# A new step table for the attention's planner, and another place for three pieces of VectorE's and ScalarE's work in the second feed-forward layer

## The chip, the cores and the metric

One core of one Trainium2 chip runs the whole program. The metric is the device time of one execution in microseconds (us), as the median of three runs. Beside it stands one profiled execution, whose trace tells when each instruction of each engine ran: PE is TensorE's matrix multiplications, PEld its weight loads, DVE is VectorE, ACT is ScalarE, POOL is GpSimd and SP is SyncE, which issues DMAs here.

## What is computed

A block-causal attention on 4 x 8 heads of 576 tokens, then two feed-forward layers on the 2304 x 512 result. The second layer multiplies its hidden values by their own cosine. Everything is float32.

```python
# attention, B, H, S, D = 4, 8, 576, 64; key blocks of 64 up to the query's own
scores = np.where(block_i >= block_j, q @ k.T / sqrt(D), -1e9)
attn = exp(scores - max(scores)); attn /= sum(attn) + 1e-9
x = (attn @ v).transpose(0, 2, 1, 3).reshape(2304, 512)
# first layer, 512 -> 2048 -> 512
g = relu(x @ w_in) ** 2;  x = g @ w_out
# second layer, 512 -> 2048 -> 512
h = x @ w2_in;  out = (h * cos(h)) @ w2_out
```

## The kernel before

**Attention (to 150.5 us in the trace).** The heads go in 16 pairs, and two pairs make one round, called Q below (8 rounds). The order of the work is not written out: `class Plan` (L56 on) holds every step with its engine, an assumed cost, a rank and what it waits for, and sends the steps out one by one, in each case the one that can start soonest, and among equals the one with the lowest rank. The rank is the pair's number on a scale plus an entry of the table `RANK`, with one row for each kind of step and five columns for early, middle and late pairs. PE's products come in three forms of its array, named by the planner's `mode`: "quarters" (64 x 64; the scores at L440 and the scores of the last key block, L488), "all" (128 x 128; the transposes of P at L601 and of the last block's PL at L628) and "columns" (128 x 64; P transposed times the values, L656). `SWITCH` and `STAY` are what the planner adds for a change of form. In one steady round PE does scores, last scores (16 products at L488), a product with 20 matmuls at L656, then the transposes of the next pairs.

**First layer.** Blocks of tokens go through x @ w_in (L1128), the squares (L1005 to L1008) and the outputs (L1062), 8 steps to a block. Its last blocks also split the second layer's weights from float32 into parts; that work is called `convert` (DVE: L285, L268, L291, L310, L279; ACT: L261, L307, L274).

**Second layer.** Four blocks of 512 tokens, each 8 steps (r = 0 to 7), and one last block of 256 tokens. Each step forms its hidden values with seven products of half the width (L997), in the order 11, s2, s1, 12, s3, 22, s4, into three PSUM banks (bank_a, bank_b, bank_c; h0, h1 and h2 in the listings). ACT copies the first product to `p1` (L1182), and DVE adds: `u2` = s2's bank plus p1, then c22 (twice), c21 and c12 (all L1185). bank_b is used by s2, s3 and 22 in turn, so PE's s3 waits until u2 has been taken out of it. Between the seven products lie 24 matmuls of the outputs (L1064) for an earlier step's waves.

The waves of a step run through DVE and ACT in halves 1 and 0: `count` (ACT, L1017), a first range step `less` (DVE, L1020), a second one `rest` (DVE, L1020 again), `size` (ACT, L1025), `cosine` (ACT, L1028), `times` (DVE, L1031), `high` (ACT, L1034) and `low` (DVE, L1037), whose result `gs` feeds the outputs. In `second_layer` count, less and rest are issued at a step's end, and size to low in the next step. In block 1 of this layer `convert` is still running, one turn a step.

At the end of a block of the first layer `finish` copies the four accumulators into `xall`, in turn by ACT and DVE (L1079); the first outputs of the second layer need those banks. The second layer's accumulators go to DRAM by way of a tile `o` (four copies by ACT, L1095). The casts and sums that make the next block's operands (`prepare`; its casts by ACT at L960) are spread over a block's steps. In the very last block ACT and DVE each copy one half of an accumulator (L1085), and DMAs carry it out (L1087, L1090).

Of the kernel before, what the change touches and what calls it, by code (L numbers as in the profile page):

```python
# [28 lines left out]
    "load": (82.8, 1611.6, 1657.9, 3246.6, 954.3),  # L29
    "k scale": (-832.1, -930.8, -388.4, 136.8, -501.4),  # L30
    "scores": (-558.9, 281.0, 420.5, -1133.4, -1153.0),
    "maximum": (1445.5, 700.8, 1063.1, 903.2, 737.5),
    "exponential": (-486.4, -1482.8, -125.1, 162.5, -1193.8),
    "last": (184.8, 21.8, 2059.4, 1402.4, 2295.1),
    "maximum last": (2758.6, 929.9, 2619.1, 1994.3, 2109.6),
    "exponential last": (1969.8, 2274.9, 3555.7, 1382.3, 1535.7),
    "guard": (-2663.2, -2893.3, -2702.3, -868.9, -2289.9),
    "invert": (-262.4, -573.8, -174.1, 303.8, -626.9),
    "scale": (-2043.2, -104.9, -614.7, 400.0, -1131.2),
    "guard last": (-1325.7, -1081.9, -491.4, -1263.7, -1854.2),  # L40
    "invert last": (236.2, 753.5, 476.9, 965.6, 609.5),
    "scale last": (679.6, -403.4, 136.8, 510.8, -90.6),
    "turn": (466.2, 1248.8, -506.4, 902.5, 824.5),
    "turned": (2175.2, 2205.7, 1749.8, 1390.3, 1533.7),
    "turn last": (-2697.6, -2953.5, -3175.8, -2666.8, -2239.3),
    "turned last": (-553.6, -1082.6, 956.0, -65.3, -20.2),
    "lesser": (-1876.9, -1222.0, -913.7, -1060.9, -1794.0),
    "value load": (-3600.7, -827.7, -2460.7, -3001.3, -2351.0),
    "weighted": (-371.1, -843.8, -605.9, 170.3, -119.5),
    "keep": (-891.0, -537.2, -248.1, -248.9, 1171.0),  # L50
    "weights": (2361.2, 4005.7, 2327.2, 3114.2, 2407.8),
# [4 lines left out]
class Plan:  # L56
# [7 lines left out]
    SWITCH = 0.15  # L64
    STAY = 0.261
# [37 lines left out]
    def emit(self):  # L103
# [16 lines left out]
        for _ in self.steps:  # L120
            best = None
            for engine, mine in able.items():
                times, rooms = {}, {}
                for n in mine:
# [6 lines left out]
                    if mode not in (None, tiling):  # L131
                        times[n] = max(times[n], clock[engine] + self.SWITCH) + self.STAY
# [43 lines left out]
def tile_block_causal_attention__then__two_ffn(  # L176
# [12 lines left out]
    nc = tc.nc  # L189
# [172 lines left out]
    def attention():  # L362
        with ExitStack() as actx:
# [67 lines left out]
            def add_scores(p, m):  # L431
# [4 lines left out]
                def product():  # L436
# [9 lines left out]
                    "P", max(0.18, (n - 64) / 600), ("scores", rank), product,  # L446
# [30 lines left out]
            def add_last(Q):  # L477
# [5 lines left out]
                for y in range(2):  # L483

                    def product(y=y):
# [8 lines left out]
                        "P", 2 * S / 2400, ("last", rank + y / 4), product, keys, [f"SL{Q}.{y}", f"free{r}.L"],  # L494
# [186 lines left out]
            def add_half(n):  # L681
# [6 lines left out]
                plan.add("A", 0.56, rank, x.shift, late, [raw])  # L688
                plan.add("V", 0.45, rank, x.mask, [high] + late, [bits], **both)
# [57 lines left out]
    def layers():  # L747
# [329 lines left out]
        def finish(layer, t0, n, a, end):  # L1077
# [4 lines left out]
            if end:  # L1082
                o = raw_p.tile([128, DM], F32, tag="raw", name="o")
                for copy, own in zip(copies, halves):
                    copy(out=o[:, own], in_=accs[a][:, own])  # L1085
                if a < n // 128 - 1:
                    nc.sync.dma_start(out=rows, in_=o)  # L1087
                    return
                for queue, own in zip((nc.scalar, nc.sync), halves):
                    queue.dma_start(out=rows[:, own], in_=o[:, own])  # L1090
                return
# [23 lines left out]
        def run(*keys):  # L1115
            for key in keys:
                if late:
                    late[key]()
# [54 lines left out]
        def second_layer(s, i, r):  # L1173
# [17 lines left out]
            run(("size", 1), ("size", 0), ("cosine", 1), ("cosine", 0))  # L1191
            times("s2", "t2", bank_b, True)
            plus(u2, bank_b, p1)
            run(("times", 1),)
# [13 lines left out]
            elif not (loads or loaded or begun) and r < half - 1 and i + 1 < len(blocks):  # L1208
                if r >= 1 and not todo and ready[0] < i:
# [9 lines left out]
            pop(len(pend) - per - 3)  # L1219
            times("22", "t4", bank_b, False)  # L1220
# [10 lines left out]
            if (loads or loaded or begun) and r == 1:  # L1231
                convert()
# [96 lines left out]
```

## Time and profile before

| | us |
|---|---|
| median of three runs (lowest, highest) | 940.26 (939.94, 942.24) |
| the profiled execution's own time | 940.51 |
| its span, first to last instruction | 938.0 |
| PE busy | 923.5 (98%) |
| DVE busy | 666.1 (71%) |
| ACT busy | 616.2 (66%) |
| attention from PE's start of its steady part to its end | 17.6 to 150.5 |
| second layer, block 1 | 537.1 to 627.9 |
| second layer, blocks 2, 3 and 4 | 627.9 to 885.9 |
| last block and the way out | 885.9 to 938.0 |

The span leaves out 2.5 us of the execution. PE is busy nearly throughout, so the time is PE's work plus the idle stretches in front of single PE instructions; these are what the rows further down look for. A busy DVE or ACT matters only where PE stands waiting at the end of what they do.

### The profile page before, as it was taken

The numbers are of one execution on the slowest core, as the hardware profiler recorded it, in microseconds if no ns is written. First come the engines' busy times: TensorE is split into PE (matmuls) and PEld (weight loads), VectorE is DVE, ScalarE is ACT, GpSimd is POOL, SyncE is SP. The second block draws the span as 40 slices with busy tenths as digits, with TensorE's granted clock in tenths as the row PEclk, the third lists the DMA queues.
The fourth block names the chain that finished last, engine by engine and source line by source line (L and its number), as shares of the span: only waits on it lengthen the run. The fifth ranks groups of instructions, "written<-read, shape, count | busy, mean of one in ns | idle before, by whom it ended". The sixth has DMA issues, their size and how long they took to land.

```text
span 938.0 us, 15762 instructions
## 1 busy us (share of the span) xinstructions
PE 923.5 (98%) x5818; PEld 783.1 (83%) x5818; DVE 666.1 (71%) x1386; ACT 616.2 (66%) x1328; POOL 93.6 (10%) x204
## 2 busy tenths in 40 slices
PE   7999999999999999999999999999999999999998
PEld 4777778888888888888888888889899889899897
DVE  6988997777786556655477567777776777666654
ACT  7987898887886556655568745565555555645564
POOL 4867741000000000000000000000000000000000
PEclk9999999999999999999999999999999999999999
DMA  8434303667665766776554754445454545554462
GB/s 308 145 134 155 120 30 112 202 206 259 202 202 199 259 237 226 242 249 228 198 180 181 265 205 156 160 158 202 171 198 182 202 165 193 184 212 157 136 217 75
DMA packets 41308, 176.12 MB, mean 188 GB/s; under 512 B 4240, under 2 KB 9616, under 8 KB 34064
## 3 DMA queue, kind: packets, MB, share of 16 engines
q1 hardware_dynamic: 40512, 174.41, 53.5%
q8 instruction: 45, 0.74, 0.3%
q10 hardware_dynamic: 720, 0.72, 0.2%
q14 instruction: 31, 0.25, 0.1%
HBM read 145.23 MB, written 29.88 MB: 187 GB/s over the span
## 4 chain that ended last, share of the span: by engine, by line
PE 89%; DVE 6%; ACT 3%; DMA 1%; issue 1%; POOL 0%; SPq 0%; ACTq 0%; DVEq 0%; POOLq 0%
PE acc L1064 18%; PE h L1128 14%; PE h L997 14%; PE acc L1062 13%; PE h L855 7%; PE acc L879 5%; PE ps L440 4%; PE ps L656 4%; PE ps L601 4%; PE h L1243 2%; PE h L879 2%; DVE g L1020 1%; DMA kB<-in_kT_dram 1%; PE ps L488 1%; DVE ha L1185 1%
## 5 line engine op out<-in xcount | busy, mean ns | idle before, releaser
L1064 PE MATMUL acc<-w,gs 128*128 128x512 f32 x864 | 221.0, 393 | 0.9 <-ACT o L1095 0.9
L1064 PEld LDWEIGHTS acc<-w,gs 128*128 128x128 f32 x864 | 153.2, 189 | 27.5 <-DVE gs L1037 1.3
L1062 PE MATMUL acc<-gs,w 128*128 128x512 f32 x576 | 138.9, 389 | 0.0
L1128 PE MATMUL h<-xs,ws 128*128 128x512 f32 x576 | 137.8, 389 | 0.0
L1128 PEld LDWEIGHTS h<-xs,ws 128*128 128x128 f32 x576 | 108.1, 188 | 22.3
L1062 PEld LDWEIGHTS acc<-gs,w 128*128 128x128 f32 x576 | 107.7, 188 | 21.9
L1008 DVE TENSOR_TENSOR gs<-ha,gs 128x512 fp32r<-128x512 f32 x48 | 33.2, 692 | 90.2 <-ACT gs L1007 90.2
L997 PE MATMUL h<-w,ws 128*128 128x256 f32 x480 | 70.8, 283 | 4.1 <-DVE u L1185 2.4
L997 PEld LDWEIGHTS h<-w,ws 128*128 128x128 f32 x480 | 65.4, 189 | 10.4 <-DVE u L1185 4.6
L1037 DVE TENSOR_TENSOR gs<-g,gs 128x512 fp32r<-128x512 f32 (+1 forms) x80 | 48.2, 635 | 32.3 <-ACT gs L1034 32.2
L307 ACT CAST w<-bits 128x512 fp32r<-128x512 f32 x64 | 39.9, 624 | 45.5 <-DVE bits L285 45.5
L855 PE MATMUL h<-xs,w 128*128 128x512 f32 (+1 forms) x384 | 68.9, 335 | 0.0
L855 PEld LDWEIGHTS h<-xs,w 128*128 128x128 f32 x384 | 59.6, 188 | 7.9
L1031 DVE TENSOR_TENSOR g<-ha,g 128x512 f32<-128x512 f32 x64 | 43.9, 687 | 29.9 <-ACT g L1028 29.9
L1017 ACT ACTIVATE turns<-ha 128x512 int32<-128x512 f32 x64 | 37.3, 626 | 41.1 <-DVE ha L1185 40.6
L1005 ACT ACTIVATE ha<-h 128x512 f32<-128x512 f32 x48 | 28.5, 593 | 50.0 <-PE h L1128 50.0
L1025 ACT ACTIVATE g<-g 128x512 f32<-128x512 f32 (+1 forms) x80 | 45.1, 588 | 22.6 <-DVE g L1020 22.6
L1182 ACT COPY ha<-h 128x256 f32<-128x256 f32 x32 | 11.9, 372 | 62.7 <-DVE g L1031 59.4
L1028 ACT ACTIVATE g<-g,half_pi 128x512 f32<-128x512 f32 (+1 forms) x80 | 50.5, 670 | 0.5
L1020 DVE SCALAR_TENSOR_TENSOR g<-turns,ha 128x512 f32<-128x512 int32 x64 | 41.6, 689 | 10.7 <-ACT turns L1017 10.7
L1020 DVE SCALAR_TENSOR_TENSOR g<-turns,g 128x512 f32<-128x512 int32 (+1 forms) x80 | 48.0, 633 | 0.6
L1185 DVE TENSOR_TENSOR ha<-h,u 128x256 f32<-128x256 f32 x96 | 37.8, 420 | 13.0 <-PE h L997 11.3
(170 smaller groups left out, 1715.7 us busy)
## 6 DMA issues: line engine op xcount, KB each, us to landing
raw<-in_w_dram SPq DMA_DIRECT2D x64, 512.0 KB, 4.4
qB<-in_qd_dram SPq DMA_DIRECT2D x15, 576.0 KB, 5.2
ws<-parts1.0_2025 SPq DMA_DIRECT2D x4, 1792.0 KB, 7.3
ws<-parts1.1_2026 SPq DMA_DIRECT2D x4, 1792.0 KB, 7.3
ws<-parts1.2_2027 SPq DMA_DIRECT2D x4, 1792.0 KB, 7.3
ws<-parts1.3_2028 SPq DMA_DIRECT2D x4, 1792.0 KB, 8.4
ws<-parts1.4_2029 SPq DMA_DIRECT2D x4, 1792.0 KB, 7.3
ws<-parts1.5_2030 SPq DMA_DIRECT2D x4, 1792.0 KB, 7.2
```

The costliest lines, as they stand in the source:

```text
L855: nc.tensor.matmul(h, lhsT=w[:, a, kk * 128 : (kk + 1) * 128], rhs=xs[kk].parts[:, y], start=(m == 0), stop=(m == 3 * KD - 1),)
L879: nc.tensor.matmul(accs[a][:, 0:n], lhsT=w[:, x, a * 128 : (a + 1) * 128], rhs=gs[:, y], start=(c == 0 and m == 0 and a % shared == 0), st ...
L997: nc.tensor.matmul(bank[:, 0:n], lhsT=w[:, c : c + 128], rhs=own[two][:, y, k, 0:n], start=(start and k == 0 and i == 0), stop=(k == 1 and ...
L1020: nc.vector.scalar_tensor_tensor(out=own, in0=turn, scalar=-part, in1=start, op0=ALU.mult, op1=ALU.add)
L1025: nc.scalar.activation(out=own, in_=own, func=AF.Abs)
L1028: nc.scalar.activation(out=own, in_=own, func=AF.Sin, bias=half_pi, scale=-1.0)
L1031: nc.vector.tensor_tensor(out=own, in0=h, in1=own, op=ALU.mult)
L1037: nc.vector.tensor_tensor(out=to[:, 1], in0=own, in1=to[:, 0].bitcast(F32), op=ALU.subtract)
L1062: nc.tensor.matmul(accs[a][:, 0:n], lhsT=w[:, y, sl], rhs=gs[:, z, x, 0:n], **flags)
L1064: nc.tensor.matmul(accs[a], lhsT=gs[:, y, x, sl], rhs=w[:, z], **flags)
L1128: nc.tensor.matmul(h[:, 0:n], lhsT=w[:, c : c + 128], rhs=xs[kk].parts[:, y], start=(m == 0), stop=(m == 3 * KD - 1),)
L1185: nc.vector.tensor_tensor(out=to, in0=bank[:, 0:m], in1=what, **add)
```

## The change

It has five parts.

1. `RANK` gets new numbers throughout, `SWITCH` becomes a table by pair of forms, `STAY` becomes 0, and the assumed costs of the scores, the last scores, and two of convert's steps are altered. PE's order is the same up to 17.6 us. After that its changes of form go from 49 to 54.
2. In block 1 of the second layer (`i == last + 1`) u2's addition is issued ahead of `rest`. In the later blocks the code moves too, but the order on every engine stays.
3. In step r = 1 of that block `convert` is issued ahead of product 22 and its addition c21, where it had been at the step's end.
4. `prepare` for the last, smaller block begins at r = 2 of block 4, not r = 1.
5. In the last block the two halves of an accumulator go into two tiles of their own, with a DMA each.

```diff
-    SWITCH = 0.15
-    STAY = 0.261
+    SWITCH = {("quarters", "columns"): 0.45, ("quarters", "all"): 0.28, ("all", "quarters"): 0.1,
+              ("all", "columns"): 0.25, ("columns", "all"): 0.12, ("columns", "quarters"): 0.12}
+    STAY = 0.0
...
-    "scores": (-558.9, 281.0, 420.5, -1133.4, -1153.0),
+    "scores": (-876.3, 699.6, 689.0, 88.7, -607.6),
...
-                    "P", max(0.18, (n - 64) / 600), ("scores", rank), product,
+                    "P", (0.18, 0.33, 0.538, 0.751)[m], ("scores", rank), product,
...
         def finish(layer, t0, n, a, end):
...
-                o = raw_p.tile([128, DM], F32, tag="raw", name="o")
-                for copy, own in zip(copies, halves):
-                    copy(out=o[:, own], in_=accs[a][:, own])
...
+                parts = [pool.tile([128, DM // 2], F32, tag=tag, name="o") for pool, tag in ((raw_p, "raw"), (bits_p, "bits"))]
+                for copy, own, o in zip(copies, halves, parts):
+                    copy(out=o, in_=accs[a][:, own])
+                for queue, own, o in zip((nc.scalar if a == n // 128 - 1 else nc.sync, nc.sync), halves, parts):
+                    queue.dma_start(out=rows[:, own], in_=o)
...
         def second_layer(s, i, r):
...
             times("11", "11", bank_a, True)
             copy(p1, bank_a)
-            run(("size", 1), ("size", 0), ("cosine", 1), ("cosine", 0))
+            if i > last + 1:
+                run(("rest", 1), ("rest", 0))
+                run(("size", 1), ("size", 0), ("cosine", 1), ("cosine", 0))
             times("s2", "t2", bank_b, True)
             plus(u2, bank_b, p1)
+            if i == last + 1:
+                run(("rest", 1), ("rest", 0))
+                run(("size", 1), ("size", 0), ("cosine", 1), ("cosine", 0))
             run(("times", 1),)
...
-                if r >= 1 and not todo and ready[0] < i:
+                if r >= (1 if blocks[i + 1][2] > 256 else 2) and not todo and ready[0] < i:
...
             pop(len(pend) - per - 3)
+            if (loads or loaded or begun) and r == 1:
+                convert()
             times("22", "t4", bank_b, False)
             plus(c21, bank_b, p1)
...
-            run(("count", 1), ("less", 1), ("count", 0), ("less", 0), ("rest", 1), ("rest", 0))
+            run(("count", 1), ("less", 1), ("count", 0), ("less", 0))
             ws.append(stream(s + 2))
-            if (loads or loaded or begun) and r == 1:
-                convert()
```

VectorE's order in a steady step of block 1, from c21 and c12 (the two additions into ha that close a step) to the first `times` (L1031 before, L1032 after); u1 is u2, and the two rows at L1020 (L1021 after) are less and rest. Before:

```order
L1185 TENSOR_TENSOR ha_2033<-h1_2042,u0_3352 128x256
L1185 TENSOR_TENSOR ha_2033<-h2_2043,u1_3353 128x256
L1020 SCALAR_TENSOR_TENSOR g_2034<-turns_2035,ha_2033 128x512 x2
L1020 SCALAR_TENSOR_TENSOR g_2034<-turns_2035,g_2034 128x512 x2
L1185 TENSOR_TENSOR u1_3353<-h1_2042,u0_3352 128x256
L1031 TENSOR_TENSOR g_2034<-ha_2033,g_2034 128x512
```

The same stretch of VectorE in the changed kernel:

```order
L1183 TENSOR_TENSOR ha_2033<-h1_2042,u0_3352 128x256
L1183 TENSOR_TENSOR ha_2033<-h2_2043,u1_3353 128x256
L1021 SCALAR_TENSOR_TENSOR g_2034<-turns_2035,ha_2033 128x512 x2
L1183 TENSOR_TENSOR u1_3353<-h1_2042,u0_3352 128x256
L1021 SCALAR_TENSOR_TENSOR g_2034<-turns_2035,g_2034 128x512 x2
L1032 TENSOR_TENSOR g_2034<-ha_2033,g_2034 128x512
```

The addition u1 has moved ahead of the two second range steps.

VectorE in step r = 1 of the same block, from the first accumulator copy into xall to the next step's u1. Before:

```order
L1079 COPY xall_60<-acc1_2046 128x512
L1185 TENSOR_TENSOR ha_2033<-h1_2042,u0_3352 128x256
L1079 COPY xall_60<-acc3_2048 128x512
L1185 TENSOR_TENSOR ha_2033<-h2_2043,u1_3353 128x256
L1020 SCALAR_TENSOR_TENSOR g_2034<-turns_2035,ha_2033 128x512 x2
L1020 SCALAR_TENSOR_TENSOR g_2034<-turns_2035,g_2034 128x512 x2
L285 SCALAR_TENSOR_TENSOR bits_5262<-raw_5169,bits_5262 128x512
L268 TENSOR_SCALAR bits_5438<-raw_5211 128x512
L291 TENSOR_SCALAR raw_5169<-bits_5262 128x512
L310 SCALAR_TENSOR_TENSOR w1_5440<-raw_5169 128x512
L279 SCALAR_TENSOR_TENSOR raw_5211<-raw_5211 128x512
L1185 TENSOR_TENSOR u1_3353<-h1_2042,u0_3352 128x256
```

The same stretch in the changed kernel:

```order
L1080 COPY xall_60<-acc1_2046 128x512
L286 SCALAR_TENSOR_TENSOR bits_5262<-raw_5169,bits_5262 128x512
L269 TENSOR_SCALAR bits_5412<-raw_5211 128x512
L292 TENSOR_SCALAR raw_5169<-bits_5262 128x512
L311 SCALAR_TENSOR_TENSOR w1_5414<-raw_5169 128x512
L280 SCALAR_TENSOR_TENSOR raw_5211<-raw_5211 128x512
L1183 TENSOR_TENSOR ha_2033<-h1_2042,u0_3352 128x256
L1080 COPY xall_60<-acc3_2048 128x512
L1183 TENSOR_TENSOR ha_2033<-h2_2043,u1_3353 128x256
L1021 SCALAR_TENSOR_TENSOR g_2034<-turns_2035,ha_2033 128x512 x2
L1183 TENSOR_TENSOR u1_3353<-h1_2042,u0_3352 128x256
L1021 SCALAR_TENSOR_TENSOR g_2034<-turns_2035,g_2034 128x512 x2
```

Convert's five instructions now stand ahead of c21 and of the copy of the accumulator acc3. On ACT, convert's three instructions have moved ahead of the two counts in the same way.

PE in one of four steady rounds of the attention, from the last scores on (ps are PSUM banks, PT the transposed P, ident the identity that transposes). Before:

```order
L488 MATMUL ps1_87<-kB1_99,qB1_97 64x288 x2
L488 MATMUL ps2_88<-kB1_99,qB1_97 64x288 x2
L656 MATMUL ps4_90<-PT_106,vB0_100 64x320 x6
L656 MATMUL ps4_90<-PT_106,vB0_100 64x192 x2
L656 MATMUL ps4_90<-PT_106,vB0_100 64x64 x2
L601 MATMUL ps0_86<-ident_94,P1_103 128x128 x3
L601 MATMUL ps3_89<-ident_94,P1_103 128x128 x2
L601 MATMUL ps5_91<-ident_94,P1_103 128x128 x3
```

The same place in the changed kernel:

```order
L489 MATMUL ps1_87<-kB1_99,qB1_97 64x288 x2
L489 MATMUL ps2_88<-kB1_99,qB1_97 64x288 x2
L602 MATMUL ps4_90<-ident_94,P1_103 128x128 x3
L602 MATMUL ps5_91<-ident_94,P1_103 128x128 x2
L657 MATMUL ps0_86<-PT_106,vB0_100 64x320 x6
L657 MATMUL ps0_86<-PT_106,vB0_100 64x192 x2
L657 MATMUL ps0_86<-PT_106,vB0_100 64x64 x2
L602 MATMUL ps3_89<-ident_94,P1_103 128x128 x3
```

Five transposes have moved between the last scores and the product with the values, so the round has one change of form more: quarters to all to columns to all, where it was quarters to columns to all.

## Rows read from the trace of the kernel before

**Rows 1.** Windows: stretch, its length, each engine's busy time, clock, DMA share, GB/s.

```profile
17.60:44.40 26.80, 26.43 (x275) 17.84 (x274) 24.83 (x71) 24.67 (x84) 20.10 (x43) 1.00 0.52 184
44.40:62.00 17.60, 17.11 (x186) 13.06 (x186) 15.81 (x45) 15.04 (x53) 13.46 (x27) 1.00 0.48 163
...
114.60:131.80 17.20, 17.20 (x190) 13.17 (x186) 15.48 (x46) 15.18 (x53) 9.22 (x21) 1.00 0.13 39
...
537.08:627.90 90.82, 86.69 (x531) 75.33 (x530) 68.27 (x129) 48.97 (x92) 0.00 (x0) 1.00 0.47 170
627.90:711.80 83.90, 83.90 (x528) 75.77 (x528) 62.74 (x117) 48.41 (x91) 0.00 (x0) 1.00 0.51 187
```

**Rows 2.** Waits of PE, whole span: total us, times, longest us.

```profile
PE h L997 <- DVE u L1185: 2.4, 5, 0.6
...
PE h L997 <- ACT u L1182: 1.6, 1, 1.6
...
PE acc L1064 <- ACT o L1095: 0.9, 1, 0.9
```

**Rows 3.** Timeline of DVE, block 1, r = 3: start, duration, work [idle before].

```profile
571.36 0.75 DVE L1185 TENSOR_TENSOR ha<-h,u 128x256 f32<-128x256 f32 x2
...
573.68 1.29 DVE L1020 SCALAR_TENSOR_TENSOR g<-turns,g 128x512 f32<-128x512 int32 x2
574.89 0.42 DVE L1185 TENSOR_TENSOR u<-h,u 128x256 f32<-128x256 f32 x1
576.28 0.69 DVE L1031 TENSOR_TENSOR g<-ha,g 128x512 f32<-128x512 f32 x1 [0.97 <-ACT g L1028]
...
582.58 0.75 DVE L1185 TENSOR_TENSOR ha<-h,u 128x256 f32<-128x256 f32 x2
```

**Rows 4.** Timeline of ACT, the same step.

```profile
574.40 1.23 ACT L1025 ACTIVATE g<-g 128x512 f32<-128x512 f32 x2 [1.19 <-DVE g L1020]
```

**Rows 5.** Waits of PE's weight loads, 537 to 628 us.

```profile
PEld acc L1064 <- DVE gs L1037: 1.1, 5, 0.2
```

**Rows 6.** Timeline of DVE, block 1, r = 1 and the start of r = 2.

```profile
547.16 1.29 DVE L1020 SCALAR_TENSOR_TENSOR g<-turns,g 128x512 f32<-128x512 int32 x2
549.59 0.42 DVE L1185 TENSOR_TENSOR u<-h,u 128x256 f32<-128x256 f32 x1 [1.14 <-PE h L997]
...
552.11 0.42 DVE L1185 TENSOR_TENSOR ha<-h,u 128x256 f32<-128x256 f32 x1 [0.53 <-PE h L997]
...
556.41 0.42 DVE L1185 TENSOR_TENSOR ha<-h,u 128x256 f32<-128x256 f32 x1
556.74 0.68 DVE L1079 COPY xall<-acc 128x512 f32<-128x512 f32 x1
...
560.33 0.68 DVE L285 SCALAR_TENSOR_TENSOR bits<-raw,bits 128x512 int32<-128x512 int32 x1
...
562.93 0.42 DVE L1185 TENSOR_TENSOR u<-h,u 128x256 f32<-128x256 f32 x1
```

**Rows 7.** Timeline of ACT, the same two steps: `size` in each.

```profile
549.08 1.16 ACT L1025 ACTIVATE g<-g 128x512 f32<-128x512 f32 x2
...
562.45 1.15 ACT L1025 ACTIVATE g<-g 128x512 f32<-128x512 f32 x2
```

**Rows 8.** Timeline of PE: the start of r = 1; s3 in r = 2.

```profile
547.91 0.86 PE L997 MATMUL h<-x,ws 128*128 128x256 f32 x6
...
562.60 0.62 PE L997 MATMUL h<-w,ws 128*128 128x256 f32 x3 [1.63 <-ACT u L1182]
```

**Rows 9.** Waits of PE's weight loads in the attention, 17.6 to 150.5 us.

```profile
PEld ps L656 <- ACT P L461: 4.1, 9, 0.8
PEld ps L440 <- issue: 2.5, 14, 0.2
```

**Rows 10.** Timeline of ACT, block 4, r = 1.

```profile
813.31 1.13 ACT L960 CAST w<-xall 128x512 fp32r<-128x512 f32 x2
814.35 2.05 ACT L1095 COPY o<-acc 128x512 f32<-128x512 f32 x4
```

**Rows 11.** Timeline of all engines at the end of the span.

```profile
934.56 0.42 DVE L1085 COPY o<-acc 128x256 f32<-128x256 f32 x1 [0.25 <-ACT o L1085]
```

More of the change, by code (lines that the diff above doesn't have):

```diff
@@ L38 @@
[L38 to L51, printed above, removed]
+    "load": (-964.0, -731.8, 2319.7, 3133.6, 468.5),
+    "k scale": (-1833.3, 1359.2, 47.9, 333.1, -120.1),
+    "scores": (-876.3, 699.6, 689.0, 88.7, -607.6),
+    "maximum": (-2621.0, -1807.0, -594.7, -1953.9, -3799.3),
@@ new lines @@
+    "exponential": (-3057.9, -3148.5, -2803.8, 191.6, -3203.5),
+    "last": (592.1, -2806.1, 1535.1, 1316.3, 2690.4),
+    "maximum last": (2712.7, 2276.8, 3848.6, 4410.1, 5047.3),
+    "exponential last": (927.5, 1454.5, 2551.6, -654.0, -50.0),
+    "guard": (-5570.2, -5786.9, -8094.5, -4110.3, -5181.2),
+    "invert": (-5145.6, -4135.8, -1703.9, 998.9, -3344.7),
+    "scale": (-3065.9, 66.6, -2886.8, 1313.2, -1759.3),
+    "guard last": (-4894.8, -3786.8, -1238.8, -3107.8, -6566.3),
+    "invert last": (-662.3, -831.5, -330.7, 404.4, 688.8),
@@ new lines @@
+    "scale last": (-1315.6, -148.9, -610.5, -1163.3, -998.9),
+    "turn": (713.4, 1849.0, -2383.8, 1343.1, 1134.3),
+    "turned": (2751.9, 1271.1, 2550.0, 210.4, 3432.6),
+    "turn last": (-5523.5, -4843.3, -4490.8, -4924.8, -5313.2),
+    "turned last": (-2149.1, -610.6, 1611.7, -3319.7, -1207.6),
+    "lesser": (-1858.7, -1745.0, 514.3, -1367.7, -3134.9),
+    "value load": (-6165.8, -2019.4, -4760.4, -4899.4, -3631.5),
+    "weighted": (1881.4, 1007.8, 323.0, 597.0, 3465.6),
+    "keep": (-1247.9, -2543.2, -390.4, -521.4, 2056.9),
@@ L52 @@
+    "weights": (4802.4, 4476.0, 5508.5, 5706.4, 5025.9),
     "cut": (1000000.0, 1000000.0, 1000000.0, 1000000.0, 1000000.0),
@@ L131, in emit @@
                     if mode not in (None, tiling):
-                        times[n] = max(times[n], clock[engine] + self.SWITCH) + self.STAY
+                        times[n] = max(times[n], clock[engine] + self.SWITCH.get((tiling, mode), 0.0)) + self.STAY
                 if times:
@@ L493, in add_last @@
                     steps.append(plan.add(
-                        "P", 2 * S / 2400, ("last", rank + y / 4), product, keys, [f"SL{Q}.{y}", f"free{r}.L"],
+                        "P", 0.57, ("last", rank + y / 4), product, keys, [f"SL{Q}.{y}", f"free{r}.L"],
                         holds=2, mode="quarters", late=0.15,
@@ L1248, in last_block @@
                 if x == 0:
-                    run(("size", 1), ("size", 0), ("cosine", 1), ("cosine", 0), ("times", 1), ("times", 0))
+                    run(("rest", 1), ("rest", 0), ("size", 1), ("size", 0), ("cosine", 1), ("cosine", 0))
+                    run(("times", 1), ("times", 0))
                     run(("high", 1), ("low", 1), ("high", 0), ("low", 0))
```

17 lines of the change are left out of this document (2 added, 15 removed).

## The prediction, made before the changed kernel had run

> **What bounds the kernel now.** I read the windows first. Where nothing holds PE, its busy time fills the stretch: blocks 2 to 4 of the second layer take 10.48 us a step, eight steps are 83.90 us, and PE is busy for all of it [rows 1]. So PE's own work sets the time there, and only its idle time and its changes of form can be won. Block 1 of the same layer does the same products in 90.82 us, 6.9 more. That is the largest loss behind the start, and the change's second and third part aim at it. The view of PE's waits names the places [rows 2]: five waits for u2 (2.4 us together), one for the copy p1 (1.6), and, in block 4, one of 0.9 for the copies into o. In the attention the windows show less: three of four steady rounds take 17.60 us and one 17.40, against 17.20 in the last steady round, where PE never waits [rows 1].
>
> A named wait is not yet a cause. For block 1 I therefore followed the loop of one step through DVE and ACT [rows 3, 4]. c21 starts at 571.36 and again at 582.58, a period of 11.22 us. Between the two, count, less, rest, size, cosine, times, c22, the second times, high, low and convert follow one another, each behind the one before, and none stands waiting for PE in r = 3 or later: size starts at 574.40, just as the first rest (573.68, 0.69 long) is over; the first times starts at 576.28 behind cosine. u2's addition at 574.89 lies beside that loop, in DVE's gap of 0.97 us before times. So in r = 3 to 7 the loop sets the pace, and PE's wait for u2 is where PE happens to be caught up with. The weight loads say the same: once past u2, PE waits again, five times and 1.1 us in all, for gs from low [rows 5].
>
> **Part 2: u2 ahead of rest (r = 3 to 7).** Nothing is added or removed; one addition moves from the gap into the loop. Its price is from start to start: an addition at 556.41 lets the next DVE instruction begin at 556.74 [rows 6], so 0.33 us. Rest, size and everything behind them come 0.33 later in each step; DVE's gap before times grows by the same. PE gets bank_b earlier and no longer waits for u2, but then waits for gs, behind which the output matmuls (L1064) and all later products queue. Five steps: 5 x 0.33 = 1.65 us longer. The lower bound is that PE's waits for u2 simply go: 2.4 shorter.
>
> **Parts 2 and 3: r = 1 and r = 2.** Here I go by clock times. In r = 1, u2 waits for PE's product s2 until 549.59, 1.68 after PE began the step at 547.91 [rows 6, 8]. Rest stood ahead of it, at 547.16, and size at 549.08 [rows 6, 7]. Now rest queues behind u2 on DVE: it starts at 549.92, and size at about 550.65, 1.57 later. Of that, c22 at 552.11 gives back some, since it waits 0.53 for PE anyway [rows 6]; I take 1.1 for what follows. Then convert's five instructions, 2.60 us on DVE (560.33 to 562.93 [rows 6]), come ahead of c21, which moves from 556.41 to 556.41 + 1.1 + 2.6 = 560.1. The copy of acc3 into xall, 556.74 before, follows at 560.45 and ends near 561.1 (0.68). This is a wait that the change adds: PE's last output matmuls of the step need that bank, and behind them on PE's queue stands the whole of r = 2. Three of them take 0.7 (83.90 us make eight steps of 24 wide and 42 half-wide matmuls, 0.233 for a wide one [rows 1]). So r = 2 starts at 561.85, its u2 1.68 later at 563.5, rest at 563.85, size at 564.6. Before, size of r = 2 came at 562.45 [rows 7], since ACT's copy p1 stood behind convert, and PE's wait of 1.63 at 562.60 [rows 8] was for that copy. That wait goes; the later start costs 564.6 - 562.45 = 2.1 us more than it gives. The bounds are 1.6 shorter, if acc3's copy holds nobody, and 2.6 longer, if c22 gives nothing back (2.1 + 1.57 - 1.1). Block 1 together: 1.65 + 2.1 = 3.75, taken as **+3.7**; between -4.0 (2.4 and 1.6 gone) and +4.7 (5 x 0.42, the addition's whole length, and 2.6).
>
> **Part 1: the attention.** PE's products are the same; their order changes from 17.6 us on, and the changes of form rise from 49 to 54, one each in five rounds. What can be won is PE's idle time: 0.37 us in the first window (26.80 less 26.43), and in the four steady rounds with the new order, from 44.40 to 114.60, their distance to 17.20: 0.4 three times and 0.2 once, 1.4 in all [rows 1]. The reason to expect some of it: with five transposes between the last scores and the product, PE has work while ACT and DVE finish that product's input. The price of a form change has two rows: a first weight load waits 2.5 / 14 = 0.18 us when the quarters form begins, and 4.1 / 9 = 0.46 when columns follow the last scores [rows 9]. The new order drops the dear one and adds two cheaper ones, so I take +0.1 net a round, near the cheap row, with 0 and 0.46 as ends. Four rounds: -1.4 + 0.4 = -1.0. The two rounds before: -0.4 for their idle time, +0.1 for the fifth change. Together **-1.3**; between -1.8 (all idle time, no price) and +2.3 (none of it, 5 x 0.46). SP's weight loads come behind two more operand loads and POOL passes some scalings to ACT; PE waits for neither of them here, and I put them at nothing. Covers that could fail are ACT's 24.67 of 26.80 and DVE's 15.81 of 17.60 us.
>
> The last scores followed by the values show a wait of 0.46 a time [rows 9]. The Trainium skill (TensorEngine Tiling (Array Packing), Tiling Modes, Key Properties) says that changing the tiling mode drains TensorE, at any change. If so, each added change costs the dear row; by my rows it costs a quarter of that. By the rule this part would be +0.5 and the whole sum 1.8 higher; the row of 0.18 speaks against it.
>
> **Part 4: prepare a step later in block 4.** Two casts on ACT (813.31 to 814.35, 1.04 us) stand ahead of the four copies into o [rows 10], and PE waits 0.86 us, shown as 0.9, for those copies [rows 2]. Without the casts the copies start 1.04 earlier, more than PE's wait. Later in the block the same two casts a step run without any wait of PE. **-0.9**; between -1.0 and 0.
>
> **Part 5: the end.** The halves have tiles of their own, but still one PSUM bank, and the last DVE copy still waits for ACT's (0.25 before it [rows 11]) in the changed order. One DMA issue more on SP falls before the last accumulator is there. **0**; between -0.3 and +0.3.
>
> **Sum.** 3.7 - 1.3 - 0.9 + 0 = +1.5 us. On the profiled execution's 940.51 (span 938.0 and 2.5 around it) that is 942.0; the median of the three runs stands 0.25 lower, at 940.26, which gives **941.8**.
>
> **Rivals.** First: PE's waits are the cause, not the loop. Then the five for u2 and the one for p1 go, 4.0 us, and the others as above: -4.0 - 1.3 - 0.9 = -6.2, 934.1 us. For it speaks that the wait view names just these two; against it, that PE waits for gs directly behind u2 [rows 5] and that c21's period has no link through PE.
>
> Second, on the slow side: each change of form empties PE at the dear row's price. Place: five rounds of the attention. Price: 5 x 0.46 = 2.3 in place of 0.5, so the sum is +3.3, 943.6 us. It decides from some 0.37 a change on, where the total passes the 2.8 us below. The rule of the Trainium skill named above would have it so; against it stands 0.18 at the start of the quarters form.
>
> Third: u2's move is free, as DVE has its gap of 0.97 to give, and PE's 2.4 us come back, while r = 1 costs what I worked out: -2.4 + 2.1 - 1.3 - 0.9 = -2.5, 937.8 us. It needs rest not to be on the path, against size starting right at rest's end [rows 3, 4].
>
> Fourth: the convert move costs nothing, as acc3's copy is early enough for PE, and p1's wait goes; u2's move costs 1.65 and 1.1. Then 1.65 + 1.1 - 1.6 - 1.3 - 0.9 = -1.0, 939.2 us. Against it, c21 and acc3's copy stand behind 2.60 us of convert in the new order.
>
> **How the numbers follow.** The forecast has a chance of 0.48, the first rival 0.13, the second 0.17, the third 0.10, the fourth 0.12. About 0.3%, 2.8 us, is what a measurement can tell from no change: faster means under 937.4, slower over 943.1. Faster is the first rival and a third of the third, 0.16. Slower is the second and a part of the forecast, where the attention gives nothing or block 1 costs its 4.7: 0.23. The rest is 0.61. The range leaves out the first rival and the far end of the second: 937.5 to 944.2.
>
> **What the new profile would show.** Right: block 1 at about 94.5 us; PE's wait for u2 gone, one for gs in its place, 0.5 to 1.5 us a step; c21's period 11.55; in r = 1 a wait of PE of some 3 us for acc3's copy; no wait for o in block 4; steady rounds near 17.3. It would be wrong if block 1 came near 84, which is the first rival, or if the attention ended later than 150.5, which is the second.

## The result: slower by 0.8%, and the profile after

| | before | after |
|---|---|---|
| median (lowest, highest; runs) | 940.10 (939.73, 942.24; 4) | 947.13 (946.41, 949.46; 4) |
| the profiled execution's own time | 940.51 | 949.46 |
| its span | 938.0 | 947.7 |

The ratio is 1.008, with a 95% interval from 1.0059 to 1.0101: 7.0 us slower. The prediction had 941.8, with a range from 937.5 to 944.2. The changed kernel's profiled execution is its slowest run, 2.3 us over its median; the first experiment shows what may lie behind that.

Where the 9.7 us between the two spans lie can be read from where PE's first products of each stage start. The attention's first product with the values starts at 19.06 (16.78 before), block 1 of the second layer at 542.44 (537.08), and block 2 at 638.64 (627.74). So 2.3 us are lost before 17 us, 3.1 in the rest of the attention and up to block 1, 5.5 in block 1, and 1.2 come back later (block 4 and the end).

Windows of the changed kernel (stretch, length, busy time of PE, PEld, DVE, ACT and POOL, granted clock, DMA share, GB/s): block 1, block 2, then r = 1, r = 2 and r = 4 of block 1, r = 1 of block 4, and a stretch of 4 us in block 1.

```profile
542.44:638.64 96.20, 89.82 (x530) 76.19 (x528) 68.17 (x129) 49.46 (x92) 0.00 (x0) 0.98 0.45 161
638.64:722.68 84.04, 84.04 (x529) 75.94 (x528) 62.90 (x118) 48.41 (x91) 0.00 (x0) 1.00 0.52 187
553.28:567.71 14.43, 11.78 (x67) 9.42 (x66) 10.11 (x20) 8.30 (x15) 0.00 (x0) 0.98 0.59 226
567.71:580.05 12.34, 12.25 (x67) 10.61 (x66) 7.65 (x14) 6.07 (x11) 0.00 (x0) 0.88 0.16 41
592.40:603.98 11.58, 10.96 (x67) 9.31 (x66) 8.75 (x17) 5.29 (x10) 0.00 (x0) 1.00 0.45 162
817.09:827.73 10.64, 10.64 (x67) 9.54 (x66) 6.50 (x13) 7.05 (x14) 0.00 (x0) 1.00 0.47 191
566.00:568.00 2.00, 1.34 (x5) 1.10 (x6) 1.84 (x5) 1.26 (x2) 0.00 (x0) 0.79 0.83 351
568.00:570.00 2.00, 2.00 (x11) 2.00 (x11) 0.39 (x1) 0.37 (x1) 0.00 (x0) 0.50 0.03 8
```

Blocks from the second on are as before (84.04 here, 83.90 in [rows 1]). Block 1 has grown by 5.5 us: r = 1 takes 14.43 (10.80 before) and the later steps 11.58 (11.21 before). The last two rows show something that no row of before has in this block: right behind r = 1's wait the granted clock falls to 0.50, that is from 2.4 to 1.2 GHz, and r = 2 runs on a mean clock of 0.88. In block 4 r = 1 takes 10.64, where it took 11.62.

Waits of PE in the changed kernel, whole span (total us, times, longest):

```profile
PE h L998 <- DVE ha L1183: 3.5, 6, 0.9
PE acc L1065 <- DVE xall L1080: 1.9, 1, 1.9
...
PE ps L657 <- ACT P L462: 1.1, 4, 0.4
...
PE acc L1065 <- ACT xall L1080: 0.7, 1, 0.7
PE h L856 <- ACT xall L666: 0.5, 1, 0.5
```

Against [rows 2], the waits for u2, for p1 and for o are gone. In their place stand six for ha (the additions c22 and c21), two for the accumulator copies into xall in r = 1 (1.9 and 0.7), four in the attention ahead of the product with the values (L657), and one ahead of the first layer (L856).

VectorE in a steady step of block 1 (start, duration, work, idle before it), to be held against [rows 3]:

```profile
580.70 0.75 DVE L1183 TENSOR_TENSOR ha<-h,u 128x256 f32<-128x256 f32 x2
581.81 1.29 DVE L1021 SCALAR_TENSOR_TENSOR g<-turns,ha 128x512 f32<-128x512 int32 x2 [0.36 <-ACT turns L1018]
583.02 0.42 DVE L1183 TENSOR_TENSOR u<-h,u 128x256 f32<-128x256 f32 x1
583.36 1.28 DVE L1021 SCALAR_TENSOR_TENSOR g<-turns,g 128x512 f32<-128x512 int32 x2
585.96 0.69 DVE L1032 TENSOR_TENSOR g<-ha,g 128x512 f32<-128x512 f32 x1 [1.31 <-ACT g L1029]
...
592.25 0.75 DVE L1183 TENSOR_TENSOR ha<-h,u 128x256 f32<-128x256 f32 x2
```

u2 at 583.02 lets rest begin at 583.36, 0.34 later. The gap before times has grown from 0.97 to 1.31, and the period from c21 to c21 from 11.22 to 11.55.

### The profile page after: what moved, and what is told of

Read it like the earlier page. It is cut to its first block, busy times and chain, and to the rows that moved or that the text cites. A ratio compares the mean times of both kernels' runs of the same rounds, so it can differ in the third digit from the quotient of the medians.

```text
span 947.7 us, 15752 instructions
## 1 busy us (share of the span) xinstructions
PE 930.3 (98%) x5818; PEld 784.4 (83%) x5818; DVE 666.2 (70%) x1385; ACT 618.3 (65%) x1331; POOL 92.2 (10%) x202
## 4 chain that ended last, share of the span: by engine, by line
PE 87%; DVE 6%; ACT 4%; issue 1%; DMA 1%; POOL 0%; SPq 0%; ACTq 0%; DVEq 0%; POOLq 0%
PE acc L1065 18%; PE h L1126 14%; PE h L998 13%; PE acc L1063 13%; PE h L856 7%; PE acc L880 5%; PE ps L657 4%; PE ps L602 4%; PE ps L441 3%; PE h L1246 2%; PE h L880 2%; ACT P L462 1%; ACT g L1026 1%; DVE g L1032 1%; DVE g L1021 1%
## 5 line engine op out<-in xcount | busy, mean ns | idle before, releaser
L998 PE MATMUL h<-w,ws 128*128 128x256 f32 x480 | 70.8, 283 | 3.6 <-DVE ha L1183 3.3
L998 PEld LDWEIGHTS h<-w,ws 128*128 128x128 f32 x480 | 65.2, 189 | 10.4 <-DVE ha L1183 6.5
L856 PE MATMUL h<-xs,w 128*128 128x512 f32 (+1 forms) x384 | 68.9, 336 | 0.5 <-ACT xall L666 0.5
L1032 DVE TENSOR_TENSOR g<-ha,g 128x512 f32<-128x512 f32 x64 | 43.9, 687 | 32.9 <-ACT g L1029 32.9
L856 PEld LDWEIGHTS h<-xs,w 128*128 128x128 f32 x384 | 59.7, 188 | 8.5 <-ACT xall L666 0.7
L1021 DVE SCALAR_TENSOR_TENSOR g<-turns,ha 128x512 f32<-128x512 int32 x64 | 41.5, 688 | 10.9 <-ACT turns L1018 10.9
L1021 DVE SCALAR_TENSOR_TENSOR g<-turns,g 128x512 f32<-128x512 int32 (+1 forms) x80 | 48.0, 632 | 0.6
L657 PE MATMUL ps<-PT,vB 128*64 128x320 f32 (+4 forms) x448 | 46.9, 361 | 1.1 <-ACT P L462 1.1
```

Of the source, the lines that this page charges most:

```text
L657: nc.tensor.matmul(plan.bank(s)[own, a - c0 : c1 - c0], lhsT=vB[x][:, j, e], rhs=PT[:, x, j, e, a:c1], start=(n == 0), stop=(n == len(todo ...
L856: nc.tensor.matmul(h, lhsT=w[:, a, kk * 128 : (kk + 1) * 128], rhs=xs[kk].parts[:, y], start=(m == 0), stop=(m == 3 * KD - 1),)
L998: nc.tensor.matmul(bank[:, 0:n], lhsT=w[:, c : c + 128], rhs=own[two][:, y, k, 0:n], start=(start and k == 0 and i == 0), stop=(k == 1 and ...
L1021: nc.vector.scalar_tensor_tensor(out=own, in0=turn, scalar=-part, in1=start, op0=ALU.mult, op1=ALU.add)
L1032: nc.vector.tensor_tensor(out=own, in0=h, in1=own, op=ALU.mult)
```

## The experiments

All medians stand beside runs of the kernel before on the same chip, which gave medians of 941.48 in the first group (26 runs; `att_only` and the three experiments with `no_att` that follow it), 941.09 in the second (23; `loop_short`, `parts45`, `loop45_late`, `att_banks`) and 942.16 in the third (22; `att_sw28`, `no_att_loop`). The first group ran on another chip than the other two. Differences are to the median of the same group.

### Part 1 alone (att_only)

The table `RANK`, `SWITCH`, `STAY` and the planner's costs as in the change; the rest as before.

```diff
-    SWITCH = 0.15
-    STAY = 0.261
+    SWITCH = {("quarters", "columns"): 0.45, ("quarters", "all"): 0.28, ("all", "quarters"): 0.1,
...
```

> The kernel before with the first part of the change alone (the new table of ranks, switches and costs in the attention). Theory A, the new order itself costs: the median is 3 to 3.5 us above the kernel before (943.1 to 943.6), and from the first product with the values (17 us) to the end of the attention the trace is about 3 us longer than before, with some 0.3 us in each of the four rounds that have five transposes between the last scores and that product. Theory B, the loss in the changed kernel's profile is TensorE's granted clock in the first 15 us, which differs from run to run: the median is within 0.7 us of the kernel before, and only the stretch up to 17 us varies.

Measured: 944.47, 3.0 us above the kernel before; ratio 1.0032 (1.0021 to 1.0044). So the new order costs 3 us by itself, as theory A had it; in the trace the attention, from the first product with the values to the first layer, takes 136.57 us against 133.75 before. Theory B can have a share in the changed kernel's profile only. The start of its attention was slow, but the order of PE is the same there in all kernels, and both speeds occur with either table. The profile's granted clock does not tell them apart: it reads 1.00 from 6 to 10 us in all four traces below, so what makes the start slow stays open. Timelines of PE, the 16 matmuls of the scores from 6 us on, in the kernel before and in `no_att` (below), both with the old tables:

```profile
6.10 1.94 PE L440 MATMUL ps<-kB,qB 64*64 64x320 f32 x16 [1.03 <-POOL kB L411]
```

```profile
6.27 3.26 PE L440 MATMUL ps<-kB,qB 64*64 64x320 f32 x16 [1.02 <-POOL kB L411]
```

And in the changed kernel and in `att_sw28` (below), with the new ones:

```profile
6.17 3.26 PE L441 MATMUL ps<-kB,qB 64*64 64x320 f32 x16 [0.93 <-POOL kB L412]
```

```profile
5.87 1.94 PE L441 MATMUL ps<-kB,qB 64*64 64x320 f32 x16 [0.63 <-POOL kB L412]
```

The first product with the values starts between 16.2 and 18.8 us in the experiments' traces, with old and new tables alike. So it varies from execution to execution. The changed kernel's profiled run has its first product at 19.06, 2.3 us later than the kernel before; that may be why it lies 2.3 us over its median, but its other runs have no trace to show it.

### Parts 2 to 5 alone (no_att)

The changed kernel with the old tables in the attention.

```diff
-    SWITCH = {("quarters", "columns"): 0.45, ("quarters", "all"): 0.28, ("all", "quarters"): 0.1,
...
+    SWITCH = 0.15
+    STAY = 0.261
```

> The changed kernel with the attention's old tables, so parts 2 to 5 alone. The loop theory (VectorE and ScalarE pace block 1, and the accumulator copy behind convert holds TensorE in step r = 1): block 1 takes 96.2 us as in the changed kernel (90.7 before), with steps of 11.55 us from r = 4 on and 14.4 us for r = 1; block 4 is 1.0 shorter and the end 0.2 shorter; the median is 944.4. Rival, TensorE's waits were the cause and the longer block came from the attention's different phase: block 1 is at 88 us or less, the median 936 or less.

Measured: 944.09, 2.6 above the kernel before; 1.0028 (1.0017 to 1.0039). Block 1 takes 94.83 us, r = 1 14.19, r = 2 11.09, r = 4 11.55 (windows of block 1, r = 1, r = 2 and r = 4):

```profile
539.66:634.49 94.83, 88.29 (x530) 74.72 (x528) 68.20 (x129) 49.47 (x92) 0.00 (x0) 1.00 0.45 162
550.51:564.70 14.19, 11.54 (x67) 9.28 (x66) 10.02 (x19) 8.09 (x15) 0.00 (x0) 1.00 0.58 227
564.70:575.79 11.09, 10.97 (x68) 9.30 (x66) 7.69 (x15) 6.28 (x12) 0.00 (x0) 1.00 0.19 51
588.13:599.68 11.55, 10.93 (x67) 9.31 (x66) 8.72 (x17) 5.28 (x10) 0.00 (x0) 1.00 0.45 163
```

The steps are as the loop theory has them; the rival fell, for the block is 4.2 longer than before, not shorter. I had expected 96.2, as in the changed kernel. The difference is r = 2: 11.09 at full clock here, 12.34 there at 0.88. The same wait in r = 1 was followed by the fall of the clock in the changed kernel but not here.

### u2 behind rest again (no_att_u2_back)

```diff
-            if i > last + 1:
-                run(("rest", 1), ("rest", 0))
-                run(("size", 1), ("size", 0), ("cosine", 1), ("cosine", 0))
+            run(("rest", 1), ("rest", 0))
+            run(("size", 1), ("size", 0), ("cosine", 1), ("cosine", 0))
             times("s2", "t2", bank_b, True)
             plus(u2, bank_b, p1)
-            if i == last + 1:
...
```

> As no_att, with u2's addition behind the second range step again in block 1. Loop theory: steps r = 4 to 7 go back to 11.22 us, the wait for u2 returns, and with r = 1's share of some 0.5 to 1.1 the median is 2.0 to 2.5 us under no_att, about 942.2. Rival, u2's place costs nothing, since VectorE has a gap of 1 us in each step: the same time as no_att within 0.5 us.

Measured: 940.35, 3.7 us under no_att and 1.1 under the kernel before (0.999, 0.9976 to 1.0003), which is not clear of noise. The steps are back at 11.25, and u2's place is worth more than my 2.0 to 2.5. In the two traces block 1 differs by 2.6 (92.26 against 94.83). In this trace the clock fell again behind r = 1's wait (r = 1 and r = 2):

```profile
549.23:562.20 12.97, 11.09 (x68) 9.37 (x66) 9.34 (x18) 7.92 (x15) 0.00 (x0) 1.00 0.58 221
562.20:574.24 12.04, 12.04 (x68) 11.00 (x66) 8.30 (x16) 6.20 (x12) 0.00 (x0) 0.86 0.22 71
```

### convert of r = 1 at the step's end again (no_att_conv_back)

```diff
-            if (loads or loaded or begun) and r == 1:
-                convert()
             times("22", "t4", bank_b, False)
...
             ws.append(stream(s + 2))
+            if (loads or loaded or begun) and r == 1:
+                convert()
```

> As no_att, with convert of step r = 1 at the step's end again. Theory: TensorE's wait of 2 us and more for the accumulator copy goes, and with it the drop of its granted clock to half right behind that wait; step r = 1 is back at 10.8 us, r = 2 takes 13.5 to 14 as its second range step waits for u2, steps r = 3 to 7 stay at 11.55; the median is 2 to 3 us under no_att, about 942. Rival, convert's place is free and all of the loss is u2's: the same as no_att within 0.5 us.

Measured: 942.78, 1.3 under no_att, 1.3 above the kernel before (1.0014, 1.0004 to 1.0023). PE's wait of 1.9 for the copy of acc3 is gone, and there is no half clock in the block. But r = 1 takes 12.02, not the expected 10.8: with u2 early, size comes late in r = 1 already, and PE waits 0.7 for ScalarE's copies into xall. Step r = 2 takes 12.41, where I had expected 13.5 to 14, and steps r = 4 to 7 stay at 11.55. So u2's early place costs 3.3 us in the block without any help (93.92 against 90.66).

### One copy out of the loop (loop_short)

The kernel before; u2 is not touched.

```diff
-            copy(c11, bank_a)
+            if i > last + 1:
+                copy(c11, bank_a)
             run(("high", 1), ("low", 1), ("high", 0), ("low", 0))
+            if i == last + 1:
+                copy(c11, bank_a)
```

> The kernel before, with one ScalarE copy in block 1 of the second layer put elsewhere: c11 is copied out of its bank after the two casts high, not before them. It waits for the second times, and in the kernel before the cast high of half 1 stands behind it for 1.6 us. u2 stays where it was. Loop theory (VectorE and ScalarE pace the block, TensorE's wait for u2 is a consequence): the loop is about 0.9 us shorter a step, steps r = 3 to 7 fall from 11.22 to TensorE's own 10.5 us, the waits for u2 go though u2 was not touched, block 1 takes 86.5 to 87.5 us in place of 90.7, and the median is 3.2 to 4 us under the kernel before. Rival (u2's own place holds TensorE): steps and median as in the kernel before within 0.5 us.

Measured: 935.30, 5.8 us under the kernel before; 0.9931 (0.9915 to 0.9947). Block 1 takes 85.62, and its steps run at PE's own 10.47 (windows of the block and of r = 4; DVE from u2 to low; ACT's casts and the copy):

```profile
537.58:623.20 85.62, 84.49 (x529) 75.74 (x528) 69.15 (x130) 50.13 (x92) 0.00 (x0) 1.00 0.50 179
...
581.31:591.78 10.47, 10.47 (x67) 9.46 (x66) 8.80 (x17) 5.67 (x12) 0.00 (x0) 1.00 0.49 181
```

```profile
583.84 0.42 DVE L1185 TENSOR_TENSOR u<-h,u 128x256 f32<-128x256 f32 x1
585.23 0.69 DVE L1031 TENSOR_TENSOR g<-ha,g 128x512 f32<-128x512 f32 x1 [0.98 <-ACT g L1028]
...
587.43 1.46 DVE L1037 TENSOR_TENSOR gs<-g,gs 128x512 fp32r<-128x512 f32 x2
```

```profile
585.96 0.62 ACT L1034 CAST gs<-g 128x512 fp32r<-128x512 f32 x1
587.54 0.62 ACT L1034 CAST gs<-g 128x512 fp32r<-128x512 f32 x1 [0.97 <-DVE g L1031]
588.07 0.37 ACT L1182 COPY ha<-h 128x256 f32<-128x256 f32 x1
```

u2 still stands behind rest, and yet no wait for it is left among PE's waits of this kernel. This settles what the wait meant: the loop was the bound, and where it is shortened PE no longer catches up with u2. Before, the copy c11 (at 578.65 in the step of [rows 3]) waited for the second times, and the cast high of the other half, whose input had long been ready, stood behind it. The gain is larger than I expected; 5.0 of the 5.8 us stand in the block (90.66 to 85.62), where r = 2 and r = 3 are shorter as well (12.36 to 11.76 and 11.66 to 10.65).

### Parts 4 and 5 alone (parts45)

```diff
-                if r >= 1 and not todo and ready[0] < i:
+                if r >= (1 if blocks[i + 1][2] > 256 else 2) and not todo and ready[0] < i:
...
+                parts = [pool.tile([128, DM // 2], F32, tag=tag, name="o") for pool, tag in ((raw_p, "raw"), (bits_p, "bits"))]
```

> The kernel before with parts 4 and 5 of the change alone (the last block's operands begun a step later; two tiles at the end). Theory: step r = 1 of block 4 takes 10.65 in place of 11.6 us, the stretch behind the last matmul is 0.2 shorter, all else as before: 1.1 to 1.2 us under the kernel before. Rival, the later preparation is missed at the start of the last block: no gain, a wait near 886 us.

Measured: 940.12, 1.0 under the kernel before; 0.9981 (0.9968 to 0.9994). The step of block 4 takes 10.58, and no wait appears at the start of the last block.

### Both, and convert left out of r = 1 (loop45_late)

The edits of loop_short and parts45, and:

```diff
-            if (loads or loaded or begun) and r == 1:
-                convert()
```

> loop_short and parts45 together, and convert left out of step r = 1, so that its turns come in r = 2, 3 and 4. Theory: the wait of 1.6 us in r = 2 for the copy p1, which stood behind convert on ScalarE, goes, and nothing takes its place as the shorter loop has room: block 1 at 84.5 to 85.5 us, the median 6 to 7 us under the kernel before. Rival: the last half of the weights comes too late, TensorE waits for w, and the gain over loop_short and parts45 (4.4 to 5.2) is lost.

Measured: 934.35, 6.7 us under the kernel before; 0.9919 (0.9902 to 0.9936). This beats both kernels. Block 1 takes 84.74, 0.9 over eight times 10.48, and PE's waits in it shrink to one of 0.3:

```profile
538.47:623.21 84.74, 84.34 (x530) 75.68 (x528) 67.58 (x128) 50.11 (x92) 0.00 (x0) 1.00 0.51 181
```

```profile
PE h L997 <- DVE u L1182: 0.3, 1, 0.3
```

### Two banks exchanged (att_banks)

att_only, and the planner's first two PSUM banks change places.

```diff
-            plan = Plan([ps.tile([128, 512], F32, name=f"ps{r}") for r in range(8)])
+            banks = [ps.tile([128, 512], F32, name=f"ps{r}") for r in range(8)]
+            plan = Plan([banks[r] for r in (1, 0, 2, 3, 4, 5, 6, 7)])
```

> att_only with the planner's first two PSUM banks exchanged, the order of all work unchanged. Theory: the new plan ends the attention with a product in the bank that the first layer's first product needs, so TensorE waits 0.5 us for ScalarE's copy out of it and starts 0.7 late; with the banks exchanged the stretch from the last transposes to the first layer falls from 5.6 to 4.9 us, and the median is 0.7 us under att_only's 3.0 above the kernel before, so 2.3 above. Rival, the wait is for the tokens that the copy delivers: unchanged.

Measured: 943.82, 2.7 above the kernel before (1.0018, 1.0006 to 1.0029); by the medians alone the 0.7 can't be told from noise. The trace tells: the attention's last products, from their start to the first layer's, in att_only and in att_banks:

```profile
148.11:153.71 5.60, 5.08 (x48) 3.10 (x48) 4.49 (x9) 4.07 (x9) 0.00 (x0) 1.00 0.12 38
```

```profile
149.19:154.20 5.01, 5.01 (x49) 3.10 (x49) 4.48 (x9) 3.58 (x7) 0.00 (x0) 1.00 0.07 21
```

Before it was 4.91. In the changed kernel the last product lands in ps0, whose copy into xall the first layer's h0 then waits for; before, it landed in ps1. So 0.6 us of the attention's loss is a bank that the plan happened to choose.

### The product ahead of the transposes again (att_sw28)

```diff
-    SWITCH = {("quarters", "columns"): 0.45, ("quarters", "all"): 0.28, ("all", "quarters"): 0.1,
+    SWITCH = {("quarters", "columns"): 0.28, ("quarters", "all"): 0.28, ("all", "quarters"): 0.1,
```

> att_only with one number of the planner changed: the cost of going from quarters to columns 0.28 in place of 0.45. The plan then puts the product with the values ahead of the transposes again in just the four steady rounds, as in the kernel before; the first two rounds and the end stay as in att_only. If a further change of form costs what the starts in att_only's trace say, 0.15 us a round, the four rounds are 0.6 us shorter together and the attention from the first product with the values to the first layer takes 136.0 (136.6 in att_only, 133.5 to 134.7 with the old tables), so most of the loss is in the first two rounds and at the end. If each change drains TensorE at the price of last scores to columns, 0.46, the four rounds are 1.8 us shorter and carry most of the loss.

Measured: 942.16, the same as the kernel before (1.0003, 0.9992 to 1.0014). The median lies nearly 3 us better against its own group than att_only's did, which ran on another chip; in the traces the attention is 1.0 shorter (135.56 against 136.57). The four rounds are 1.3 shorter together, between the 0.6 and the 1.8 expected, and the two rounds ahead of them 0.5 longer. Two of these rounds in att_only, and the same two in att_sw28:

```profile
70.78:88.33 17.55, 17.32 (x189) 13.06 (x187) 15.45 (x45) 14.19 (x53) 12.23 (x26) 1.00 0.43 139
88.33:106.51 18.18, 17.39 (x188) 12.90 (x186) 15.43 (x45) 14.19 (x53) 12.20 (x26) 1.00 0.42 136
```

```profile
70.21:87.31 17.10, 17.10 (x188) 13.09 (x187) 15.12 (x45) 14.25 (x53) 12.14 (x26) 1.00 0.44 143
87.31:105.15 17.84, 17.14 (x188) 12.93 (x186) 15.07 (x45) 14.23 (x53) 12.14 (x26) 1.00 0.41 138
```

The first of them costs 0.45 more with the transposes between. Where it goes is in the timeline of PE, att_only and then att_sw28:

```profile
77.19 1.50 PE L489 MATMUL ps<-kB,qB 64*64 64x288 f32 x16
78.62 0.77 PE L602 MATMUL ps<-ident,P 128*128 128x128 f32 x5
79.62 2.27 PE L657 MATMUL ps<-PT,vB 128*64 128x320 f32 x20 [0.23 <-ACT P L462]
81.83 4.04 PE L602 MATMUL ps<-ident,P 128*128 128x128 f32 x35
85.80 2.60 PE L441 MATMUL ps<-kB,qB 64*64 64x64 f32 x40
```

```profile
76.63 1.50 PE L489 MATMUL ps<-kB,qB 64*64 64x288 f32 x16
78.06 2.27 PE L657 MATMUL ps<-PT,vB 128*64 128x320 f32 x20
80.26 4.59 PE L602 MATMUL ps<-ident,P 128*128 128x128 f32 x40
84.78 2.60 PE L441 MATMUL ps<-kB,qB 64*64 64x64 f32 x40
```

The last scores take 1.43 us to the next form, whichever it is (77.19 to 78.62, 76.63 to 78.06). The 40 transposes take 4.52 in one piece, and 1.00 + 3.97 in two, so the new order costs 0.45 and drops nothing. But the 1.00 holds an idle time of 0.23 ahead of the product. It ends with this instruction of ACT in att_only, over at 79.57, 0.05 before the product starts at 79.62:

```profile
79.35 0.22 ACT L462 ACTIVATION_READ_ACCUMULATOR P<-ps,nmax3.0_110 128x1 f32 x1
```

This is the end of an exponential that reads scores from a PSUM bank. The product does not read its result P; what it needs is the bank. The change's listing shows why: in the old order the product is formed in ps4, in the new one the transposes have taken ps4 and it gets ps0, the bank that this exponential reads in att_only's program. Each of the four rounds has such a wait in att_only; att_sw28 has none, and keeps the two for PT, ahead of the scores (PE's waits, att_only and then att_sw28):

```profile
PE ps L657 <- ACT P L462: 1.0, 4, 0.3
```

```profile
PE ps L441 <- DVE PT L636: 1.2, 2, 0.7
```

So at least 0.23 of the 0.45 is a wait for a bank, and at most 0.22 is left for the added change of form itself, which fits the 0.15 expected and not the 0.46.

### u2 early in a loop that is not the bound (no_att_loop)

no_att with loop_short's edit.

> no_att with the copy c11 behind the casts in block 1, as in loop_short. Loop theory: u2's early place lengthens a loop that is no longer the bound, so it costs nothing there: steps r = 4 to 7 take 10.5 us (11.55 in no_att, 10.47 in loop_short), while r = 1 still takes some 14 us for convert and the copy of acc3; block 1 at 88 to 89.5 us, the median 5 to 6 us under no_att's. Rival, u2's early place holds TensorE by itself: steps stay over 11 us.

Measured: 938.86, 3.3 under the kernel before (0.997, 0.9958 to 0.9983), and 5.9 better against it than no_att was. Block 1 takes 90.69, over the 88 to 89.5 expected. Its steps take 10.85, neither 10.5 nor over 11:

```profile
597.85:608.70 10.85, 10.73 (x67) 9.38 (x66) 8.83 (x16) 6.54 (x13) 0.00 (x0) 1.00 0.48 172
```

That is 0.70 under no_att's 11.55, where I had put the copy's share at 0.9. The shortened loop is then 11.22 - 0.70 = 10.52, level with PE's 10.48, and u2's 0.33 would then still come on top; that is worked out, not tried. Step r = 1 takes 13.26, with the wait of 1.8 for acc3's copy and the half clock behind it.

## Why the prediction was wrong

**Block 1, r = 3 to 7: right.** The loop, its period of 11.55 and the end of the wait for u2 came as written, and loop_short shows that the loop was the bound. Only the name of the new wait was wrong: PE stands before product 22, whose bank c22 has yet to clear (L998 behind ha), not before gs. [rows 5] are waits of weight loads, which overlap the products; no matmul of the kernel before waits for gs.

**Block 1, r = 1 and 2: right in kind, short in size.** The copy of acc3 behind convert's 2.6 us holds PE, for 1.9 us and not some 3, with 0.7 before it for ACT's copies; r = 2 starts 14.43 us after r = 1 (13.94 by my times). For both steps together I had 2.1 us more; without the half clock it is 10.80 + 12.36 before against 14.19 + 11.09 in no_att, again 2.1. But r = 3 carries another 0.7 (12.34 against 11.66), twice what I gave it. In the changed kernel's trace the clock adds 1.25 in r = 2, which no term of mine had. So +3.7 became 4.2 without the clock's fall and 5.5 with it.

**Part 4: right.** 10.64 against 11.62, 1.0 us; predicted 0.9.

**Part 5: nearly.** The DVE copy still waits 0.25 for ACT's, as forecast. The stretch from that copy's start to the end of the span is 3.22, against 3.43 before [rows 11], a gain of 0.2 that I had not counted.

**The attention: wrong, in size and in sign.** Predicted -1.3, measured +3.0 in att_only: 4.3 of the 5.3 us between the forecast and the measured time. In att_only's trace the attention is 2.8 longer than before: 1.1 in the first two rounds, 0.9 in the four steady ones (71.19 against 70.31), 0.2 behind them and 0.7 at the end. Four steps failed.

- "The new order drops the dear one and adds two cheaper ones": it drops nothing. The 0.46 [rows 9] belongs to leaving the last scores, whatever follows. Even by its own rows the step gave 2 x 0.18 - 0.46 = -0.1; the +0.1 was chosen. The changes of form alone cost at most 0.22 a round, nearer to that +0.1 than to the 0.46. The Trainium skill (TensorEngine Tiling (Array Packing), Tiling Modes, Key Properties) says that changing the tiling mode drains TensorE. The traces agree that the added change costs something, but not that it costs the dear row.
- "PE has work while ACT and DVE finish that product's input": the prediction looked at the product's input and not at its bank. The transposes ahead of it take the bank that it had before, and PE waits for ACT to clear another, 1.0 us in the four rounds of att_only and 1.1 in the changed kernel. No term of the sum had this wait.
- "Their distance to 17.20" can be won: the idle time of those rounds does not stand at the product but before the scores, where PE waits for VectorE's copies of PT. It stays with either order: att_sw28 has the old order there and still two waits for PT, 1.2 us together, and its rounds take 17.84 and 17.10 in turn with the same work.
- The first two rounds, from which I expected 0.3: in att_only they take 17.91 and 17.82, against 17.41 and 17.25 before. The last scores are split there, eight matmuls ahead of a product or the transposes and eight behind, and PE waits 0.5 for ScalarE's PL in the first. Together 1.1 us; how the split and the wait share it was not tried.

The end of the attention, 0.7, was in no term: I compared the orders by the kind of work and not by the bank it lands in.

The two halves measured apart, 3.0 and 2.6, give 5.6 of the 7.0, just inside the interval of the 7.0 (5.5 to 9.5). What else there is may be the clock's fall in r = 1, which came in some executions and not in others, and the groups of runs, between which the kernel before itself differs by 2.1 us (940.10 to 942.16); this is not settled.

Of the rivals, the first fell with loop_short, where the waits for u2 went and u2 had not been touched. The third fell with no_att_conv_back, where u2's early place alone costs 3.3 us in the block. The fourth fell with PE's wait of 1.9 for acc3's copy. The second had a price of 0.46 a round, and 0.45 was measured, but that is chance: at least half of it is the wait for a bank, and the added change of form cost less than half of the rival's price.

One thing doesn't fit. att_sw28 keeps the loss in the first two rounds and at the end, and its attention is 1.2 to 2 us longer in the trace than with the old tables (135.56 against 133.5 to 134.3 in most), yet its median equals that of the kernel before. Whether its start is faster on average was not settled. Nor was a plan tried that keeps the transposes ahead of the product and gives the product another bank, so the share of the bank in the four rounds is read from the trace alone.

## What to carry to other kernels

When PE waits for one result in every step, follow the period of that result round the other engines before moving it: if the loop has no link through PE, moving the awaited instruction lengthens it, and taking any instruction out of the loop, here a copy that an idle cast stood behind, gives the time back. Before counting a change of TensorE's form as saved, see whether the form that is left is still left somewhere: here leaving the last scores cost the same, whichever form followed. Of a new order, read also which PSUM bank each moved product gets and who has yet to empty it, and which banks its last results land in, since the next stage may begin in one of them.

## What the runs showed of the hardware that I had not expected

The granted clock falls in mid-kernel, not only at the start. In three of four traces in which PE waited 1.8 us or more for acc3's copy in r = 1, the clock went from 2.4 to 1.2 GHz right behind it (0.50 from 568 to 570 us in the changed kernel), and r = 2 took 12.0 to 12.3 us; in no_att, after the same wait, it did not fall, and r = 2 took 11.1. None of the other traces shows it in this block. So a wait of 1.8 to 1.9 us was followed by a loss of another 1 us or so, but not each time.

The start of an execution varies by more than 2 us with the same order of work: the same 16 matmuls took 1.94 or 3.26 us from 6 us on, with either kernel's tables. A single profile says nothing of a change's worth in the first 20 us.
